# One fused kernel (attention, dense MLP, routed experts): queries and keys loaded one token per partition, one copy and quartered score products per attention unit, weight low parts on VectorE, and a new plan of the order

## The chip, the cores and the metric

The kernel runs on one core of one Trainium2 chip. The metric is the device time of one execution in microseconds (us), lower is better. In the profile PE is TensorE (the matrix unit; PEld is its weight load), DVE is VectorE, ACT is ScalarE, POOL is GpSimd, and SP is SyncE, which here only starts DMAs.

## What is computed

Three layers follow each other. All inputs and outputs are float32; 2304 tokens (4 sequences of 576) have 8 heads of 64 numbers, 512 in all.

```
scores = q @ k.T / 8                       # per head
mask   = (0 <= pos_q - pos_k < 64)         # a sliding window of 64 keys
attn   = softmax(where(mask, scores, -1e9))
x      = attn @ v                          # 2304 x 512
h = x @ w_in                               # 512 -> 2048
g = where(h > 0, h, exp(min(h, 0)) - 1)
x = g @ w_out                              # 2048 -> 512
e = argmax(x @ w_gate + modality_bias[modality_id])      # one of 8 experts per token
out = gate * (relu(x @ w1[e]) @ w2[e])     # 512 -> 1024 -> 512
```

## The kernel before, in words

**Attention** is done in 36 units. Unit n is tile t = n // 2 of 128 tokens with four of the eight heads. A unit passes through these pieces (names as in the planner): `ld` and `lv` start the loads of k, q and v on SP's queue; `1p` transposes k and q on TensorE; `1k`, `1l`, `1q`, `1r` copy the result from PSUM into buffers KB (192 keys wide: the 64 keys before the tile and its 128) and QB; `2p` makes the scores; `2d` adds the mask and takes the maximum (VectorE, L387) and scales the maximum (L389); `2x` is the exponential with its sum (ScalarE, L396); `2n` the reciprocal (L402, L403); `2m` multiplies by it on GpSimd (L408); `3p`, `3a` transpose the probabilities (L428) and copy them (L433); `4p` multiplies by v; `4a`, `4d` split the result into a rounded part xh and the rest xl (L451, L456). After `2p`, GpSimd copies the last 64 keys to the front of KB for the next tile (`kw`, L415 to L421). There are two probability buffers, so two units are on the way at a time.

The k and q of a unit are loaded with two neighbouring tokens on one partition, k on partitions 0 to 63 and q on 64 to 127, in pieces of 512 bytes. The first 12 units (`pair`) are transposed into pairs of heads, by a transpose (L324) and a product with the identity (L325) for each head, and their scores are products of quarters of the array (64 rows by 64 columns, L373). The other 24 units are transposed whole (L327), copied in eight smaller copies (four on ScalarE L335, four on VectorE L337), and their scores are four full products (L377).

**The dense layer** works in groups g of 256 tokens (four units) and steps s of 256 of the 2048 hidden features, 72 steps in all. `f1` is x times w_in (L531 to L533: high times high, low times high, high times low), `fx`, `fe`, `fm` the activation (L563 or L561, L567, L571), `fh` rounds it (L575), `fl` takes the rest on GpSimd (L579), and `f2` is the product with w_out (L540 to L542). Both weight matrices are prepared once and stay resident. Each of the 16 pieces (8 of each matrix) is loaded as 8-byte numbers and made into float32 in two halves: `wa` on ScalarE (L484), three bit operations on VectorE (`wb`: L491, L493, L496), the rounded high part (`wc`, on ScalarE for the first 8 of 32 halves and on VectorE for the other 24, L337 CAST), and the low part (`wd`) on GpSimd (L514). A step needs its two pieces of w_in and w_out. So the first two groups go through the 16 steps at the pace at which weights are made; later groups find them ready.

**Gate and experts** follow: `g1` computes the gate's logits on VectorE (L609), tokens are sorted by expert, and nine slots of 256 or 384 tokens go through their expert's weights (`e1`, `e2`).

**What sets the order.** The program is a list of pieces, each with an engine, a cost, what it needs, a rank and buffers that it takes and frees. `plan` (L18) plays these through as engines that do one piece at a time, and the instructions are written in the order in which it starts them. Nothing else of the plan is in the program: each engine runs its own list in order, with semaphores for data and buffers only. So a wrong cost or a contention that the plan does not know shows as an engine that waits behind a blocked instruction. Where TensorE would sit idle before time 40 of the plan, products of the identity with itself (`fill`, L1190) are put in.

## Time and profile before

| | us |
|---|---|
| median of three runs | 817.78 |
| the three runs | 817.78, 805.19, 818.21 |
| span of the profiled execution, first to last instruction (its own time is not given beside it) | 806.1 |
| busy: PE / DVE / ACT / POOL | 769.9 / 508.1 / 329.6 / 265.3 |

The profile is of one execution. Its span lies 0.9 us above the fastest run and 12.1 us below the slowest. Three stages are told apart below by the start of two matmuls: A, to the first dense step (0 to 49.75 us); B, the 16 steps of the first two groups (to 190.5 us); C, the other 56 steps, the gate and the experts. In a table of windows, a row gives the stretch and its length, then the busy time (and number of instructions) of PE, PEld, DVE, ACT and POOL, the granted TensorE clock as a share, the mean busy share of the 16 DMA engines, and GB/s. A group's row gives line, engine, operation, output<-inputs, shapes and count, then the busy time and the mean of one in ns, then the idle time of the engine before it with what ended it. A row of the timeline gives start, duration, engine, line, operation and count.

### The profile page before, as it was taken

What the parts mean: (1) busy time and instruction counts of PE and PEld (TensorE: products, weight loads), DVE (VectorE), ACT (ScalarE), POOL (GpSimd) and SP (SyncE); (2) the same over time, 40 slices, a digit from 0 to 9 for tenths busy, and PEclk for the clock granted to TensorE, in tenths of its full rate; (3) what the DMA queues carried; (4) which work ended last, traced back from release to release, by engine and by line L of the source; (5) the groups of instructions that cost most, each with busy time, mean ns of one, the idle gap of its engine ahead of it and who ended that gap; (6) DMA issues with size and microseconds to landing.
All of it is one profiled execution on the core that took longest, in us unless ns stands there. A gap on an engine that the chain in (4) does not pass through costs nothing. (4 is left out here: it accounts for less than half of the span.)

```text
span 806.1 us, 14932 instructions
## 1 busy us (share of the span) xinstructions
PE 769.9 (96%) x5440; PEld 675.5 (84%) x5440; DVE 508.1 (63%) x1508; ACT 329.6 (41%) x818; POOL 265.3 (33%) x263
## 2 busy tenths in 40 slices
PE   9998978799999999999999999999999999999996
PEld 5676867688889899889889888898889999999995
DVE  2689899996988759559569569165876223522210
ACT  2666644444334364564553555234521112411211
POOL 2356565572342432332333324224214112100001
PEclk9999998989999999999999999999999999999998
DMA  7367881212002022121221110002605610100001
GB/s 195 104 178 224 248 323 55 66 27 79 27 7 73 14 54 67 40 76 31 40 74 33 41 40 2 1 27 60 229 1 178 214 54 29 54 22 6 27 27 41
DMA packets 82337, 62.30 MB, mean 77 GB/s; under 512 B 46577, under 2 KB 69251, under 8 KB 82123
## 3 DMA queue, kind: packets, MB, share of 16 engines
q1 hardware_dynamic: 78635, 51.50, 21.7%
q0 software_dynamic: 3616, 9.72, 3.6%
q8 instruction: 45, 0.74, 0.4%
q14 instruction: 41, 0.34, 0.2%
HBM read 51.05 MB, written 10.42 MB: 76 GB/s over the span
## 5 line engine op out<-in xcount | busy, mean ns | idle before, releaser
L531 PE MATMUL h<-xh,whi 128*128 128x256 f32 x576 | 167.2, 290 | 0.0
L533 PE MATMUL h<-xh,wlo 128*128 128x256 f32 x576 | 163.5, 284 | 1.0 <-POOL wlo L514 1.0
L532 PE MATMUL h<-xl,whi 128*128 128x256 f32 x576 | 163.5, 284 | 0.0
L579 POOL TENSOR_TENSOR g<-e,g 128x512 fp32r<-128x512 f32 x72 | 101.0, 1404 | 170.6 <-ACT g L575 158.2
L540 PE MATMUL y<-whi,g 128*128 128x512 f32 x288 | 118.7, 412 | 4.9 <-ACT g L575 4.9
L542 PE MATMUL y<-whi,g 128*128 128x512 f32 x288 | 114.7, 398 | 3.6 <-POOL g L579 3.6
L541 PE MATMUL y<-wlo,g 128*128 128x512 f32 x288 | 113.5, 394 | 0.0
L531 PEld LDWEIGHTS h<-xh,whi 128*128 128x128 f32 x576 | 110.9, 192 | 2.6 <-PE p_rk L637 0.7
L532 PEld LDWEIGHTS h<-xl,whi 128*128 128x128 f32 x576 | 111.0, 193 | 1.1
L533 PEld LDWEIGHTS h<-xh,wlo 128*128 128x128 f32 x576 | 110.8, 192 | 1.2 <-POOL wlo L514 1.2
L609 DVE CUSTOM_DVE_ANT_0 lgs<-ysb,wgb 128x512 bf16<-128x512 f32 x96 | 77.7, 810 | 1.9
L575 ACT ACTIVATE g<-e 128x512 fp32r<-128x512 f32 x72 | 45.3, 630 | 73.5 <-DVE e L571 70.6
L531 PE MATMUL h<-xh,ehi 128*128 128x256 f32 x256 | 72.6, 283 | 0.6 <-ACT xh L900 0.6
L532 PE MATMUL h<-xl,ehi 128*128 128x256 f32 x256 | 72.6, 284 | 0.6 <-DVE xl L910 0.6
L533 PE MATMUL h<-xh,elo 128*128 128x256 f32 x256 | 72.5, 283 | 0.0
L940 DVE SCALAR_TENSOR_TENSOR g<-h,g 128x512 fp32r<-128x512 f32 x32 | 22.1, 689 | 77.2 <-ACT g L935 77.1
L396 ACT ACTIVATE sm<-sm,st 128x128 f32<-128x128 f32 x144 | 56.2, 392 | 34.2 <-DVE st L389 34.1
L542 PEld LDWEIGHTS y<-whi,g 128*128 128x128 f32 x288 | 54.8, 190 | 18.1 <-POOL g L579 5.8
L571 DVE SCALAR_TENSOR_TENSOR e<-e,h 128x512 f32<-128x512 f32 x72 | 49.1, 683 | 30.8 <-ACT e L567 25.2
L540 PEld LDWEIGHTS y<-whi,g 128*128 128x128 f32 x288 | 55.1, 191 | 15.1 <-ACT g L575 5.8
L567 ACT ACTIVATE e<-e 128x512 f32<-128x512 f32 x72 | 45.3, 629 | 47.7 <-DVE e L563 47.0
L935 ACT ACTIVATE g<-h 128x512 fp32r<-128x512 f32 x32 | 19.1, 596 | 109.6 <-PE h L533 104.8
(226 smaller groups left out, 1607.0 us busy)
## 6 DMA issues: line engine op xcount, KB each, us to landing
raw<-in_moe_w_in_dram SPq DMA_DIRECT2D x16, 512.0 KB, 5.6
raw<-in_moe_w_out_dram SPq DMA_DIRECT2D x16, 512.0 KB, 5.6
wraw<-in_moe_w_dram SPq DMA_DIRECT2D x16, 512.0 KB, 12.1
v<-in_v_dram SPq DMA_DIRECT2D x58, 128.0 KB, 2.7
kq<-in_k_dram SPq DMA_DIRECT2D x28, 128.0 KB, 3.0
kq<-in_q_dram SPq DMA_DIRECT2D x28, 128.0 KB, 3.1
yd<-ysb SPq DMA_DIRECT2D x12, 256.0 KB, 2.9
wgb<-wgt SPq DMA_DIRECT2D x1, 2048.0 KB
```

The source lines that it names most:

```text
L396: act(out=sm[:, h], in_=sm[:, h], func=AF.Exp, bias=st[:, 1, h:h + 1], scale=0.125, accum_out=st[:, 2, h:h + 1])
L531: mm(hs[c], w[0][:, d, f], xh, start=d == 0, stop=False)
L532: mm(hs[c], w[0][:, d, f], xl, start=False, stop=False)
L533: mm(hs[c], w[1][:, d, f], xh, start=False, stop=d == 3)
L540: mm(y, gh[:, m], w[0][:, c], start=first and c == 0, stop=False)
L541: mm(y, gh[:, m], w[1][:, c], start=False, stop=False)
L542: mm(y, gl[:, m], w[0][:, c], start=False, stop=last and c == 1)
L567: act(out=e, in_=e, func=AF.Exp, scale=-1.0 if on_act(g) else 1.0)
L571: dve.scalar_tensor_tensor(out=e, in0=e, scalar=-1.0, in1=H.pop((g, s)), op0=ALU.add, op1=ALU.max)
L575: act(out=a[:, 0], in_=EL[g, s], func=AF.Copy)
L579: pool.tensor_tensor(out=a[:, 1], in0=EL.pop((g, s)), in1=a[:, 0], op=ALU.subtract)
L609: dve.tensor_tensor_reduce(out=lgs, in0=y, in1=wgb[:, e], scale=1.0, scalar=0.0, op0=ALU.mult, op1=ALU.add, accum_out=GT[t][:, e:e + 1])
```

## The change

One copy of `ld` and `1p` serves all units now: k and q are loaded one token per partition, in pieces of 256 bytes, each unit is transposed whole by four transposes, and one copy on ScalarE (`1e`) puts k and q into KQ, which holds the unit's tile and the tile before it (two slots, t % 2). So nothing has to be copied from one tile to the next (`kw`, `qz` are gone). The scores of all units are products of quarters of the array (`2p`, L357 in the changed kernel), into two PSUM buffers of pool ps. The scaling of the maximum is folded into the mask instruction, so L389 goes. Of the 32 weight halves, the low part of 26 is taken on VectorE (LE) and that of 6 on GpSimd; the high part of 28 is cast on ScalarE and that of 4 on VectorE (HE). The first six dense steps write the activation back into PSUM and take its low part on VectorE (VIA). `fx` runs on ScalarE in seven groups of nine in place of four (FXA). The planner gets other costs, ranks and edges, and a resource L of one piece at a time, which the two-input pieces of GpSimd and VectorE take. It is only in the plan; no instruction waits for it.

```diff
-    KQC = 0.73
-    NPR = 12
-    QE = 'ACT'
-    KE = 'DVE'
-    G1R = 45.66
-    XBL = 8.0
-    SGL = -10.97
-    SG = 9.4
+    KQC = 1.2
+    G1R = 35.77
+    XBL = 6.5
+    SGL = 4.46
+    SG = 26.38
     FG = 0.3
...
-    LV = -19.5
-    UR = (0.71, 1.24)
-    HE = range(8, 32)
-    FXA = (1, 4, 7, 8)
-    YX = (1, 6, 7)
-    LG = 6.36
+    LV = -20.92
+    UR = (0.63, 2.97)
+    HE = range(28, 32)
+    LE = range(26)
+    VIA = range(6)
+    E1 = "ACT"
+    FXA = (1, 2, 3, 4, 6, 7, 8)
+    YX = (1, 2, 6, 7)
+    LG = 16.15
...
-    LOOK = 12
-    EK = ("ACT", "ACT", "DVE", "DVE")
+
+    L = {"L": 1}
...
-        u["kq"] = u["kq"].rearrange("p j h d -> p (j h d)").rearrange("p (h x d) -> p h x d", x=2, d=D)
-        # two tokens next to each other on a partition: k on partitions 0:64, q on 64:128
         for j, src in enumerate((k, q)):
-            for off, n, b, s in runs(t * 128, 128):
-                nc.sync.dma_start(out=u["kq"][64 * j + off // 2:64 * j + (off + n) // 2].rearrange("p h x d -> p h (x d)"),
-                                  in_=src[b, 4 * qd:4 * qd + 4, s:s + n, :].rearrange("h (p x) d -> p h (x d)", x=2))
+            load(u["kq"][:, j], src, t * 128, qd)
...
         for j in range(4):
-            if pair(t, qd):
-                x = a[:, j // 2 * 2:j // 2 * 2 + 2, j % 2]
-                T(p[0:64, j], x[:, 0], ident)
-                mm(p[64:128, j], x[:, 1], ident, start=True, stop=True)
-            else:
-                T(p[:, j], a[:, j].rearrange("p x d -> p (x d)"), ident)
...
+            T(p[:, j], a[:, j // 2, j % 2 * 2:j % 2 * 2 + 2].rearrange("p h d -> p (h d)"), ident)
...
-    # head by head: rows 0:64 hold the window of queries 0:64, rows 64:128 that of queries 64:128
-    def a1k(t, qd, b, eng):
-        p, K = U[t, qd]["p1"], KB[qd]
-        for x, r in enumerate(HALF):
-            put(eng, even_odd(K[HALF[b], :, 64 - 64 * b:192 - 64 * b], x), p[r, :, 0:64])
...
-    # the first units: pairs of heads as the transposes leave them, one product per head and half of the queries
-    def pair(t, qd):
-        return 2 * t + qd < NPR
-
-    def a1kk(t, qd, eng):
-        put(eng, even_odd(KB[qd][:, 0:2, 64:192]), U[t, qd]["p1"].rearrange("p (i x) c -> p i x c", x=2)[:, :, :, 0:64])
-
-    def a1qq(t, qd, eng):
-        put(eng, even_odd(QB[qd][:, 0:2, :]), U[t, qd]["p1"].rearrange("p (i x) c -> p i x c", x=2)[:, :, :, 64:128])
...
+    def a1e(t, qd, eng):
+        put(eng, KQ[qd][:, :, t % 2], U[t, qd].pop("p1"))
+
+
+    def window(t, qd, z, i, b):
+        a = KQ[qd][HALF[z], i]
+        if b:
+            return a[:, t % 2]
+        a = a.rearrange("p s (x c) -> p (s x) c", x=2)
+        return a[:, 1:3] if t % 2 else a[:, 0:4:3]
...
     def a2p(t, qd):
         u = U[t, qd]
-        p = u["p2"] = ps.tile([128, 4, 128], F32, tag="ps", name="p_s")
-        if pair(t, qd):
-            # the halves of the array work side by side, each on a bank of its own
-            p = u["p2"] = p, h_tile().rearrange("p a b -> p (a b)").rearrange("p (a b) -> p a b", b=128)
-            for i in range(2):
-                for b, r in enumerate(HALF):
-                    for z in range(2):
-                        mm(p[z][r, i], QB[qd][HALF[z], i, r], KB[qd][HALF[z], i, 64 * b:64 * b + 128],
-                           start=True, stop=True)
-            return
-        for h in range(4):
-            mm(p[:, h], QB[qd][:, h], KB[qd][:, h, 0:128], start=True, stop=True)
+        p = u["p2"] = [ps.tile([128, 2, 128], F32, tag="ps", name="p_s") for _ in range(2)]
+        for i in range(2):
+            for b, r in enumerate(HALF):
+                for z in range(2):
+                    mm(p[z][r, i], KQ[qd][HALF[z], 2 + i, t % 2, r], window(t, qd, z, i, b), start=True, stop=True)
...
         for h in (2 * i, 2 * i + 1):
-            src = p[h % 2][:, h // 2] if pair(t, qd) else p[:, h]
-            dve.tensor_tensor_reduce(out=sm[:, h], in0=src, in1=masks[:, mask_of(t), :], scale=1.0, scalar=-3.0e38,
-                                     op0=ALU.add, op1=ALU.max, accum_out=st[:, 0, h:h + 1])
-        dve.tensor_scalar(out=st[:, 1, 2 * i:2 * i + 2], in0=st[:, 0, 2 * i:2 * i + 2],
-                          scalar1=-0.125, scalar2=None, op0=ALU.mult)
+            dve.tensor_tensor_reduce(out=sm[:, h], in0=p[h % 2][:, i], in1=masks[:, mask_of(t), t % 2], scale=-0.125,
+                                     scalar=3.0e38, op0=ALU.add, op1=ALU.min, accum_out=st[:, 0, h:h + 1])
...
-            act(out=sm[:, h], in_=sm[:, h], func=AF.Exp, bias=st[:, 1, h:h + 1], scale=0.125,
-                accum_out=st[:, 2, h:h + 1])
+            act(out=sm[:, h], in_=sm[:, h], func=AF.Exp, bias=st[:, 0, h:h + 1], scale=-1.0,
+                accum_out=st[:, 1, h:h + 1])
...
-    def akw(t, qd):
-        K = KB[qd]
...
-        pool.tensor_copy(out=K[0:64, :, 0:64], in_=K[0:64, :, 128:192])
...
-        pool.tensor_tensor(out=lo[:, c], in0=CV[kind, i][:, z].bitcast(F32), in1=hi[:, c], op=ALU.subtract)
...
+        eng = pool if lo_eng(kind, i, z) == "POOL" else dve
+        eng.tensor_tensor(out=lo[:, c], in0=CV[kind, i][:, z].bitcast(F32), in1=hi[:, c], op=ALU.subtract)
+
+    def lo_eng(kind, i, z):
+        return "DVE" if (2 * i + (kind == "o")) * 2 + z in LE else "POOL"
...
+    def via_psum(g, s):
+        return g * NP + s in VIA
...
     def f1m(g, s):
         e = EL[g, s]
-        dve.scalar_tensor_tensor(out=e, in0=e, scalar=-1.0, in1=H.pop((g, s)), op0=ALU.add, op1=ALU.max)
+        h = H[g, s] if via_psum(g, s) else H.pop((g, s))
+        dve.scalar_tensor_tensor(out=h if via_psum(g, s) else e, in0=e, scalar=-1.0, in1=h, op0=ALU.add, op1=ALU.max)
...
     def f1h(g, s):
         a = G[g, s] = g_tile()
-        act(out=a[:, 0], in_=EL[g, s], func=AF.Copy)
+        act(out=a[:, 0], in_=H[g, s] if via_psum(g, s) else EL[g, s], func=AF.Copy)
 
     def f1l(g, s):
-        a = G[g, s]
-        pool.tensor_tensor(out=a[:, 1], in0=EL.pop((g, s)), in1=a[:, 0], op=ALU.subtract)
+        a, e = G[g, s], EL.pop((g, s))
+        if via_psum(g, s):
+            dve.tensor_tensor(out=a[:, 1], in0=H.pop((g, s)), in1=a[:, 0], op=ALU.subtract)
+        else:
+            pool.tensor_tensor(out=a[:, 1], in0=e, in1=a[:, 0], op=ALU.subtract)
...
+            w2p = [("2p", n - 2)] if back else []
+
+            room = [("f1", n // 4 - 3, NP - 1)] if n >= 12 else []
+            add(("1p", n), "PE", 0.55, a1p, *u, rank=r - 1000, deps=[("ld", n)] + w2p + room,
+                need={"ps": 1}, free={} if early else {"ld": 1}, lat=0.25)
+            e = e1_eng(n)
+            add(("1e", n), e, 0.49 if e == "ACT" else 0.6, a1e, *u, e, rank=r, deps=[("1p", n)] + w2p, free={"ps": 1})
+            add(("2p", n), "PE", 0.7, a2p, *u, rank=r - 1000, deps=[("1e", n)], need={"ps": 2, "P": 1}, lat=0.25)
             for i in range(2):
-                add(("2d", n, i), "DVE", 0.475, a2d, *u, i, rank=r, deps=[("2p", n) if i == 0 else ("2d", n, 0)],
-                    free=({"ps": 1} | ({"h": 1} if pair(*u) else {})) if i else {})
+                add(("2d", n, i), "DVE", 0.53, a2d, *u, i, rank=r, deps=[("2p", n) if i == 0 else ("2d", n, 0)],
...
-            add(("2n", n), "DVE", 0.17, a2n, *u, rank=r, deps=[("2x", n, 0), ("2x", n, 1)])
-            add(("2m", n), "POOL", 1.0, a2m, *u, rank=r, deps=[("2n", n)])
-            if t + 1 < NTILE:
-                add(("kw", n), "POOL", 0.55 if pair(units[n][0] + 1, qd) else 0.97, akw, *u, rank=r + 0.5, deps=[("2p", n)])
...
+            add(("2m", n), "POOL", 1.05, a2m, *u, rank=r, deps=[("2n", n)], need=L, free=L)
...
-                        deps=[("wb",) + w + (z, x - 1) if x else ("wa",) + w + (z,)], free={"w": 1} if x == 2 else {})
-                add(("wc",) + w + (z,), hi_eng(*w, z), 0.52 if hi_eng(*w, z) == "ACT" else 0.34, w_c, *w, z, rank=r,
-                    deps=[("wb",) + w + (z, 2)] + ([("wc",) + w + (0,)] if z else []), need={} if z else {"w": 2})
-                add(("wd",) + w + (z,), "POOL", 1.23, w_d, *w, z, rank=r, deps=[("wc",) + w + (z,)],
-                    free={"w": 1} if z else {})
...
+                        deps=[("wb",) + w + (z, x - 1) if x else ("wa",) + w + (z,)], need=L, free=L | ({"w": 1} if x == 2 else {}))
+                lk = L if he == "DVE" else {}
+                add(("wc",) + w + (z,), he, 0.52 if he == "ACT" else 0.34, w_c, *w, z, rank=r,
+                    deps=[("wb",) + w + (z, 2)] + ([("wc",) + w + (0,)] if z else []), need=lk | ({} if z else {"w": 2}), free=lk)
+                add(("wd",) + w + (z,), le, 1.23 if le == "POOL" else 0.6, w_d, *w, z, rank=r, deps=[("wc",) + w + (z,)],
+                    need=L, free=L | ({"w": 1} if z else {}))
...
+                if via:
+                    add(("fl",) + k, "DVE", 0.6, f1l, *k, rank=r - 900, deps=[("fh",) + k], free={"h": 1})
+                else:
+                    add(("fl",) + k, "POOL", 1.23, f1l, *k, rank=r - 900, deps=[("fh",) + k], need=L, free=L | {"e": 1})
...
         caps = {"w": 33, "ps": 4, "h": 2, "y": 1, "P": 2, "v": 3, "ld": 2, "PA": 1, "X": 3, "e": 2, "g": 3,
-                "gs": 3, "ix": 5}
+                "gs": 3, "ix": 5, "L": 1}
```

The order itself comes out of the planner. On TensorE, the stretch after the score products of the first two units stands so before (p_t is the transposed unit, kqv its loaded k, q and v, kb and qb the buffers KB and QB; a unit's transposes are eight matmuls):

```order
L373 MATMUL h<-kb_110,qb_108 64x128
L324 MATMUL p_t<-ident,kqv 64x128
L325 MATMUL p_t<-ident,kqv 64x128
L324 MATMUL p_t<-ident,kqv 64x128
L325 MATMUL p_t<-ident,kqv 64x128
L324 MATMUL p_t<-ident,kqv 64x128
L325 MATMUL p_t<-ident,kqv 64x128
L324 MATMUL p_t<-ident,kqv 64x128
L325 MATMUL p_t<-ident,kqv 64x128
L1190 MATMUL fill<-ident 128x128 x2
```

and so in the change (L331 transposes, L357 scores, L393 the probabilities' transposes, L407 the product with v):

```order
L357 MATMUL p_s<-kq_108 64x128 x8
L331 MATMUL p_t<-ident,kqv 128x128 x4
L1165 MATMUL fill<-ident 128x128 x4
L331 MATMUL p_t<-ident,kqv 128x128 x4
L393 MATMUL p_a<-ident,sm 128x128 x4
L357 MATMUL p_s<-kq_107 64x128 x8
L407 MATMUL p_o<-PA,kqv 64x64 x8
```

Each unit's eight transposes in two forms became four in one form; the order of the units is the same. The first dense step stands after nine units' transposes before, after eight in the change.

On VectorE, a stretch in which weights are made stands so before (wf is the float32 under construction, raw the loaded numbers, whi the high part, qb a copy of q for a unit, e the activation):

```order
L563 TENSOR_SCALAR e<-h 128x512
L337 CAST whi<-wf 128x512
L491 TENSOR_SCALAR wf<-wf 128x512
L337 COPY qb_107<-p_t 64x4x32 x2
L493 SCALAR_TENSOR_TENSOR wf<-raw,wf 128x512
L571 SCALAR_TENSOR_TENSOR e<-e,h 128x512
L496 SCALAR_TENSOR_TENSOR wf<-raw,wf 128x512
```

and so in the change (L456, L458, L461 are the bit operations, L480 the low part wlo, L548 the activation, L421 the rest xl of a unit):

```order
L421 TENSOR_TENSOR xl<-p_o,xh 128x2x128
L548 SCALAR_TENSOR_TENSOR e<-e,h 128x512
L461 SCALAR_TENSOR_TENSOR wf<-raw,wf 128x512
L480 TENSOR_TENSOR wlo<-wf,whi 128x512
L458 SCALAR_TENSOR_TENSOR wf<-raw,wf 128x512
L480 TENSOR_TENSOR wlo<-wf,whi 128x512
L461 SCALAR_TENSOR_TENSOR wf<-raw,wf 128x512
L456 TENSOR_SCALAR wf<-wf 128x512 x2
```

The casts and the copies of q have left VectorE's list, and the low parts stand in it, and between the last bit operation of a half and its low part stand two to 17 other instructions.

On GpSimd, the list in the same stage stands so before (g is the activation's low part, sm the probabilities):

```order
L514 TENSOR_TENSOR wlo<-wf,whi 128x512 x2
L579 TENSOR_TENSOR g<-e,g 128x512
L514 TENSOR_TENSOR wlo<-wf,whi 128x512
L421 COPY kb_109<-kb_109 64x4x64
L514 TENSOR_TENSOR wlo<-wf,whi 128x512 x2
L579 TENSOR_TENSOR g<-e,g 128x512
```

and so in the change (L480 the low parts that stay, L559 g, L385 the probabilities):

```order
L385 TENSOR_TENSOR sm<-sm,st 128x512
L559 TENSOR_TENSOR g<-e,g 128x512 x3
L480 TENSOR_TENSOR wlo<-wf,whi 128x512 x2
L559 TENSOR_TENSOR g<-e,g 128x512
L480 TENSOR_TENSOR wlo<-wf,whi 128x512
L559 TENSOR_TENSOR g<-e,g 128x512
L480 TENSOR_TENSOR wlo<-wf,whi 128x512 x2
```

Most low parts and all copies of keys are gone from it.

## Rows read from the trace of the kernel before

**Rows 1.** The page's first line.

```profile
span 806.1 us, 14932 instructions
```

**Rows 2.** Windows of the stages A, B and C.

```profile
0.00:49.75 49.75, 46.48 (x403) 29.93 (x403) 25.44 (x113) 24.89 (x87) 18.04 (x35) 1.00 0.59 157
49.75:190.50 140.75, 124.56 (x922) 105.25 (x922) 128.63 (x281) 72.23 (x182) 81.67 (x73) 0.95 0.49 152
190.50:806.10 615.60, 598.88 (x4120) 540.31 (x4118) 354.04 (x1115) 232.44 (x551) 165.59 (x155) 1.00 0.18 54
```

**Rows 3.** Waits in stage A: total us, times, longest.

```profile
DVE kb L337 <- PE p_t L325: 17.8, 7, 6.3
```

**Rows 4.** Timeline of TensorE: score products of three pairs of units.

```profile
13.22 0.47 PE L373 MATMUL p_s<-kb,qb 64*64 64x128 f32 x1
...
22.91 0.32 PE L373 MATMUL p_s<-kb,qb 64*64 64x128 f32 x1
...
32.70 0.32 PE L373 MATMUL p_s<-kb,qb 64*64 64x128 f32 x1
```

**Rows 5.** Timeline of TensorE: transposes of a paired unit, what follows, and a plain unit's.

```profile
53.46 0.30 PE L324 MATMUL p_t<-ident,kq 128*64 128x128 f32 x1
...
55.84 0.66 PE L428 MATMUL p_a<-ident,sm 128*128 128x128 f32 x4
...
109.22 0.60 PE L327 MATMUL p_t<-ident,kq 128*128 128x128 f32 x4
```

**Rows 6.** Groups by shape, whole run: score products, 12 paired and 24 plain units.

```profile
L377 PE MATMUL p_s<-kb,qb 128*128 128x128 f32 x192 | 27.5, 288 | 5.0 <-DVE qb L337 4.9
...
L373 PE MATMUL p_s<-kb,qb 64*64 64x128 f32 x96 | 8.7, 307 | 0.0
```

**Rows 7.** Window from the first to the last activation product of stage B.

```profile
57.40:181.90 124.50, 108.31 (x781) 92.26 (x782) 119.60 (x249) 64.03 (x157) 76.23 (x68) 0.95 0.51 160
```

**Rows 8.** Groups of VectorE, 57 to 182 us.

```profile
L496 DVE SCALAR_TENSOR_TENSOR wf<-raw,wf 128x512 int32<-128x512 int32 x28 | 24.2, 868 | 0.1
L493 DVE SCALAR_TENSOR_TENSOR wf<-raw,wf 128x512 int32<-128x512 int32 x28 | 23.6, 852 | 0.1
L491 DVE TENSOR_SCALAR wf<-wf 128x512 int32<-128x512 int32 x27 | 20.6, 770 | 1.0 <-ACT wf L484 0.9
L337 DVE CAST whi<-wf 128x512 fp32r<-128x512 f32 x24 | 18.0, 748 | 0.0
L571 DVE SCALAR_TENSOR_TENSOR e<-e,h 128x512 f32<-128x512 f32 x16 | 10.9, 680 | 0.3
L389 DVE TENSOR_SCALAR st<-st 128x2 f32<-128x2 f32 x14 | 6.6, 469 | 0.5
...
L337 DVE COPY qb<-p_t 64x128 f32<-64x128 f32 x16 | 4.6, 287 | 0.2
```

**Rows 9.** Timeline of VectorE.

```profile
101.73 1.67 DVE L493 SCALAR_TENSOR_TENSOR wf<-raw,wf 128x512 int32<-128x512 int32 x1
...
104.05 0.69 DVE L496 SCALAR_TENSOR_TENSOR wf<-raw,wf 128x512 int32<-128x512 int32 x1
104.66 0.42 DVE L491 TENSOR_SCALAR wf<-wf 128x512 int32<-128x512 int32 x1
```

**Rows 10.** Timeline of GpSimd at the same time.

```profile
101.55 1.30 POOL L514 TENSOR_TENSOR wlo<-wf,whi 128x512 fp32r<-128x512 f32 x1 [0.36 <-DVE whi L337]
```

**Rows 11.** Groups of GpSimd, 57.4 to 181.9 us.

```profile
L514 POOL TENSOR_TENSOR wlo<-wf,whi 128x512 fp32r<-128x512 f32 x28 | 41.4, 1478 | 24.4 <-DVE whi L337 19.9 <-ACT whi L335 4.2 <-DMA kq<-in_k_dram 0.4
L579 POOL TENSOR_TENSOR g<-e,g 128x512 fp32r<-128x512 f32 x15 | 21.9, 1460 | 15.5 <-ACT g L575 15.5
```

**Rows 12.** Group of ScalarE, whole run: a copy of 128x512 from PSUM.

```profile
L433 ACT ACTIVATE PA<-p_a 128x512 f32<-128x512 f32 x36 | 21.4, 595 | 29.1 <-PE p_a L428 29.1
```

**Rows 13.** Waits, whole run: low parts behind high parts cast on ScalarE.

```profile
POOL wlo L514 <- ACT whi L335: 6.5, 3, 4.2
```

**Rows 14.** DMA issues: count, KB each, median us from issue to landing.

```profile
v<-in_v_dram SPq DMA_DIRECT2D x58, 128.0 KB, 2.7
kq<-in_k_dram SPq DMA_DIRECT2D x28, 128.0 KB, 3.0
```

More of the change, by code (lines that the diff above doesn't have):

```diff
@@ L150, in fused @@
     ident = const.tile([128, 128], F32, name="ident")
-    masks = const.tile([128, 3, 128], F32, name="masks")
-    QB = [const.tile([128, 4, 128], F32, name=f"qb{i}") for i in range(2)]
-    KB = [const.tile([128, 4, 192], F32, name=f"kb{i}") for i in range(2)]
+    masks = const.tile([128, 3, 2, 128], F32, name="masks")
+    KQ = [const.tile([128, 4, 2, 128], F32, name=f"kq{i}") for i in range(2)]
     wgb = const.tile([128, E, DM], F32, name="wgb")
@@ L310, in u_v @@
         load(a[:, 1], v, t * 128, qd)
+        if t % 2:
+            load(a[:, 0], v, t * 128 - 64, qd)
+            return
+        load(a[0:64, 0], v, t * 128, qd)
         if t:
-            load(a[:, 0], v, t * 128 - 64, qd)
+            load(a[64:128, 0], v, t * 128 - 64, qd)
         else:
-            pool.memset(a[0:64, 0], 0.0)
-            nc.sync.dma_start(out=a[64:128, 0], in_=v[0, 4 * qd:4 * qd + 4, 0:64, :].rearrange("h p d -> p h d"))
+            pool.memset(a[64:128, 0], 0.0)
     def a1p(t, qd):
@@ L1063, in program @@
+            add(("4a", n), "ACT", 0.28, a4a, *u, rank=r,
                 deps=[("4p", n)] + ([("4a", n - 1)] if n % 4 else []))
@@ L1086, in program @@
                 yb = {"ps": 2} if g == 1 else {"y": 1}
-                add(("f1",) + k, "PE", 2.6, f1p, *k, rank=r + 1.5,
-                    deps=[("wd", "i", s, 0), ("wd", "i", s, 1)] + [("4d", 4 * g + x) for x in range(4)] + ([("f1", g, s - 1)] if s else [("f1", g - 1, NP - 1)] if g == NG - 1 else []),
+                via = via_psum(g, s)
+                add(("f1",) + k, "PE", 2.9, f1p, *k, rank=r + 1.5,
+                    deps=[("wd", "i", s, 0), ("wd", "i", s, 1)] + [("4d", 4 * g + x) for x in range(4)] + ([("f1", g, s - 1)] if s else [("f1", g - 1 - (g < NG - 1), NP - 1)] if g > 1 else []),
                     need={"h": 1}, free=({"X": 1} if s == NP - 1 else {}) | ({"w": 2} if g == NG - 1 else {}), lat=0.22)
@@ L1136, in program @@
             add(("eh", j), "ACT", 0.95, e_hi, j, rank=j - 600.0, deps=[("el", j)], need={"w": 2})
[L1137 removed]
+            add(("ex", j), "DVE", 1.14, e_lo, j, rank=j - 600.0, deps=[("eh", j)], need=L, free=L)
         for s in range(NS):
```

108 lines of the change are left out of this document (40 added, 68 removed).

## The prediction, on record before the changed kernel ran

> **What bounds the kernel now.** I read the windows by stage first. In stage C TensorE is busy for 598.9 of 615.6 us [rows 2]: there only TensorE's own work counts, and little of its time is idle. In stage B it is busy for 124.6 of 140.8 us, 16.2 us idle, at a mean granted clock of 0.95, so part of its busy time is at the lower of its two levels, 1.2 in place of 2.4 GHz; in stage A, 3.3 us of 49.75 are idle, but with the planner's `fill` products among the busy ones. So the time that can come back lies in A and B, and in work that TensorE no longer does.
>
> Stage B next. From its first to its last activation product VectorE is busy for 119.6 of 124.5 us [rows 7], ScalarE for 64, GpSimd for 76: VectorE sets the pace at which weights, and with them steps, become ready. Much of that busy time is not work. The reader is to see in the timeline an L493 that took 1.67 us from 101.73 on, beside a GpSimd low part that ran from 101.55 for 1.30 us [rows 9, 10]; of two that nothing disturbed, the same kind took 0.69 and L491 took 0.42. The groups show it in their means: 868, 852 and 770 ns for the three bit operations and 748 ns for the cast, while L571, which has one input in PSUM, stays at 680 [rows 8]. So VectorE instructions whose tensors are all in SBUF stand still while GpSimd runs.
>
> Stage A last. VectorE waited 17.8 us in seven waits for a unit's transposes [rows 3]. The score products of pairs of units start at 13.22, 22.91 and 32.70 us [rows 4]: a loop of 9.7 us for two units, and the transposes of one paired unit hold TensorE from 53.46 to 55.84, 2.38 us, those of a plain one 0.60 us [rows 5]. A loop contains two such sets.
>
> **The change, part by part.** Durations are those of the profiled execution, so the sum is made against its span of 806.1 us [rows 1]. Its own time is not listed; the runs of 805.19, 817.78 and 818.21 us lie 0.9 us below to 12.1 above that span, so what lies around a span, or differs between executions, is bounded by these two.
>
> *Transposes, stage A.* Nine paired units stand before the first step; each becomes 2.38 - 0.60 = 1.78 us cheaper, 16.0 us in all. If all of it were on the path, A would shorten by 16 (and by up to 18 if the ninth unit's set, now behind the first step, goes whole). The wait of 17.8 us [rows 3] says that most of it is. Against that, ScalarE, busy for 24.9 us in A [rows 2], must now do the copy of each unit whole, 0.595 us [rows 12], where VectorE and ScalarE shared it, and the exponentials, the normalisation and the loads stay in the loop. I take 12, between bounds of 4 and 18, nearer to the row of the wait. There are fewer `fill` products; they stand in idle time and cost nothing.
>
> *VectorE, stage B.* Removed: 20 of the 24 casts, 20 x 0.748 = 15.0 us; all L389, 6.6; the copies of q, 4.6; together 26.2 [rows 8]. Added: 26 low parts. Their nearest row is the bit operation of the same size with two inputs, 0.61 us from start to start (104.05 to 104.66, rows 9), so 15.9 us; and six low parts of the activation, 3.7; together 19.6. Stalls of what stays: L491 27 x (0.770 - 0.42) = 9.5, L493 28 x (0.852 - 0.69) = 4.5, L496 28 x (0.868 - 0.69) = 5.0, together 19.0 us [rows 8, 9]. GpSimd ran 28 + 15 two-input pieces there [rows 11]; 6 low parts and 9 activation parts stay, 15 of 43, so I let 65% of the stalls go, 12.3 us, and let the new low parts pay the rest at the same rate, 26 x 0.17 x 0.35 = 1.6. Hand-offs: the high part of 20 more halves now comes from ScalarE between two pieces of VectorE. When GpSimd waited for a high part from ScalarE it waited 6.5 us in 3 times, 2.2 each [rows 13]. In the new order between two and 17 other VectorE instructions stand between a half's last bit operation and its low part, six in the median (counted in the order), and ScalarE, idle for half of the stage [rows 7], has a cast of that size (0.595, rows 12) done in about the time of one. I take 0.2 each, 5 us for 26, between 0 and the 57 that 2.2 would make. Sum: -26.2 + 19.6 - 12.3 + 1.6 + 5 = -12.3 us, bounded by -25 and, without any relief, +3. While VectorE is the bound, B shortens by this; what is late next is TensorE's own work of the stage. The lower clock follows TensorE's idle stretches, so its cost goes with them and I add no term.
>
> *GpSimd, DMA and SP.* GpSimd loses 26 low parts of 1.478 us [rows 11] and all copies of keys; it only released others. SP issues the same two DMAs per unit for k and q, moved past no queue that feeds a step, and one more short one for v in even tiles. A page says otherwise of the pieces: the Trainium skill, "DMA: Bandwidth & Descriptors", section Specifications, wants at least 512 B for line rate, and the change goes from 512 to 256 B. The rows point the other way: v, already in 256-byte pieces, lands after 2.7 us, k in 512-byte pieces after 3.0, for the same 128 KB [rows 14]. I take nothing; the rule's case is a rival below.
>
> *Stage C.* The score products of a plain unit take 27.5 / 24 = 1.15 us, of a paired one 8.7 / 12 = 0.73 [rows 6]. Some 20 of the 24 plain units lie in C, where TensorE is the bound: 20 x 0.42 = 8.4, taken as 8. The copies, L389, `kw` and the move of `fx` to ScalarE are hidden there under TensorE (VectorE is busy for 354 of 615.6 us, ScalarE for 232); without that cover nothing of them would be dearer than before. Three units that stood before the 17th step now stand behind it; that moves TensorE's work from B to C, and I count it as zero. The new edges and ranks hold attention back more; the 16.7 us of idle time in C could grow or shrink, +-6.
>
> Sum: 806.1 - 12 - 12 - 8 = 774 us of span. With 3 us for what the runs show around it I forecast **777 us**, 5.0% under the median of 817.78 and 3.5% under the fastest run. About 2% is what a measurement of this kernel can tell from no change.
>
> **The rivals.** *1. The lock stays.* The resource L is only in the plan; no wait in the program keeps GpSimd and VectorE apart, and drift of a microsecond undoes it. For it: that L493 started 0.18 us after the GpSimd piece [rows 9, 10]. Against it: there are 65% fewer such pieces whatever the order. Without relief B changes by -26.2 + 19.6 + 5 + 4.4 (26 x 0.17) = +3, and the span is 806 - 12 + 3 - 8 = 789, as time 789 to 801.
>
> *2. Small pieces are slow.* If k and q took twice as long to land, 6.0 in place of 3.0 us, each of three loops of stage A would wait 3 us more: 783 of span, 783 to 795. Rows 14 speak against it. This is what "DMA: Bandwidth & Descriptors" of the Trainium skill would make of the change.
>
> *3. Slower: VectorE waits for ScalarE's casts.* VectorE does its list in order. If each of the 26 low parts blocks it for the 2.2 us of [rows 13], every bit operation and activation behind it waits too: 57 us in place of 5, 774 + 52 = 826 us. It decides from 2 us per hand-off on, where the gain is lost and 2% with it ((806 + 16 - 774) / 26 + 0.2). For it: ScalarE takes 20 casts more and all unit copies. Against it: it is idle for half of the stage, and at least two other VectorE instructions stand between.
>
> *4. More comes back.* All of the transposes (16 to 18 us in A) and all stalls: then TensorE itself bounds stage B. 806 - 17 - 22 - 8 = 759 us.
>
> **How the numbers follow.** The forecast has 65%, rival 1 13%, rival 2 5%, rival 3 3%, rival 4 14%. The predicted time is that of the forecast, 777. The range runs from 756, below rival 4, to 800, near the end of rival 1; it leaves out about 2 in 10: rival 3, and the outer ends of the bounds of A and of stage C. Faster by over 2% (under 801 against the median): forecast, rivals 2 and 4 and half of rival 1, 90%; within 2%: the rest of rival 1 and a little of the others, 7%; slower: rival 3, 3%.
>
> **What would show it.** Stage A: the first dense step near 38 us, the loop of two units near 7, and VectorE's wait for transposes at a few us. Stage B: 16 steps in about 128 us, VectorE's bit operations at means near 0.45 for the shift and 0.75 for the other two, low parts near 0.7, and a clock of 1.00. Stage C: near 608 us. I would be wrong if the first step still came after 45 us (then transposes were not on the path), if VectorE's list showed waits for ScalarE's casts of over 20 us, if the means stayed at 0.77 and 0.86, or if TensorE waited in stage C for attention units that the new edges hold back.

## The result: 5.0% was forecast, 4.4% came, by other terms than mine

The changed kernel takes **774.5 us** (median of four runs, 773.49 to 776.23). The kernel before took 813.3 us in the four runs beside it (805.19 to 818.21). The ratio is **0.956, 95% interval 0.951 to 0.961**. The forecast was 777 us, the range 756 to 800. The span of the profiled execution went from 806.1 [rows 1] to 773.2 us, 32.9 us less; it took 775.0 us itself, 1.8 more than its span. One reservation for the experiments: the profile of e7 is of an execution slower than its other runs (832.6 us, their median 826.8), so its stage lengths are told and nothing rests on them alone.

First the three stages of the changed kernel, in the columns of [rows 2]; the 17th dense step starts at 138.67.

```profile
span 773.2 us, 14786 instructions
...
0.00:29.18 29.18, 24.98 (x313) 20.53 (x313) 15.96 (x83) 22.30 (x77) 12.76 (x27) 1.00 0.86 210
29.18:138.67 109.49, 102.88 (x795) 89.43 (x792) 101.17 (x216) 68.05 (x154) 34.88 (x24) 1.00 0.61 186
138.67:773.20 634.53, 610.01 (x4425) 541.54 (x4425) 316.83 (x1017) 237.24 (x561) 164.70 (x144) 0.99 0.20 56
```

Stage A is 20.6 us shorter (forecast 12), stage B 31.3 (forecast 12.3), and stage C is **18.9 us longer** (forecast 8 shorter). The total came out right because these misses cancel, which is luck.

In stage A VectorE's wait for transposes is gone. What answers to [rows 3] is, in the waits up to 29.18 us, a wait of VectorE for score products and one of ScalarE for the transposes:

```profile
DVE sm L367 <- PE p_s L357: 7.3, 3, 5.7
ACT kq L335 <- PE p_t L331: 5.0, 3, 3.2
```

The longest of the first, 5.7 us, is at the start, before there is any unit. TensorE's timeline shows the loop of two units: 5.8 and 5.9 us, then 8.5, where [rows 4] had 9.7 and 9.8, and a unit's transposes take 0.66, where [rows 5] had 2.38.

```profile
6.01 0.74 PE L357 MATMUL p_s<-kq 64*64 64x128 f32 x16
6.69 0.66 PE L331 MATMUL p_t<-ident,kqv 128*128 128x128 f32 x4
...
11.79 0.67 PE L357 MATMUL p_s<-kq 64*64 64x128 f32 x16
...
17.72 0.67 PE L357 MATMUL p_s<-kq 64*64 64x128 f32 x16
...
25.17 0.72 PE L331 MATMUL p_t<-ident,kq 128*128 128x128 f32 x4 [0.89 <-DMA kq<-in_k_dram]
...
26.25 0.67 PE L357 MATMUL p_s<-kq 64*64 64x128 f32 x16
```

The third loop is the one in which TensorE waited for a load, 0.89 us at 25.17.

In stage B these groups of VectorE (29.18 to 138.67) answer to [rows 8], and those of GpSimd to [rows 11]:

```profile
L458 DVE SCALAR_TENSOR_TENSOR wf<-raw,wf 128x512 int32<-128x512 int32 x30 | 22.1, 743 | 0.0
L461 DVE SCALAR_TENSOR_TENSOR wf<-raw,wf 128x512 int32<-128x512 int32 x30 | 20.5, 691 | 0.0
L480 DVE TENSOR_TENSOR wlo<-wf,whi 128x512 fp32r<-128x512 f32 x24 | 20.5, 863 | 0.0
L456 DVE TENSOR_SCALAR wf<-wf 128x512 int32<-128x512 int32 x30 | 12.9, 452 | 3.1 <-ACT wf L449 3.1
...
L337 DVE CAST whi<-wf 128x512 fp32r<-128x512 f32 x4 | 3.0, 755 | 0.0
```

```profile
L559 POOL TENSOR_TENSOR g<-e,g 128x512 fp32r<-128x512 f32 x8 | 20.9, 2613 | 35.0 <-ACT g L552 35.0
L385 POOL TENSOR_TENSOR sm<-sm,st 128x512 f32<-128x512 f32 x6 | 7.4, 1233 | 33.9 <-DVE st L380 17.3 <-ACT whi L335 10.6 <-ACT wf L449 4.0
L480 POOL TENSOR_TENSOR wlo<-wf,whi 128x512 fp32r<-128x512 f32 x5 | 6.7, 1337 | 7.8 <-PE p_t L331 7.8
```

The shift's mean fell from 770 to 452 ns and the last bit operation's from 868 to 691: that stall is nearly gone. The new low parts, at 863, are dearer than the 0.61 us I took: undisturbed they take 0.68, and some still stand behind a GpSimd piece, as at 64.76, in the timelines of VectorE and of GpSimd. The mean of 2613 ns of GpSimd's `g` hides two pieces of some 6 us; the last section comes to them.

```profile
63.55 0.68 DVE L480 TENSOR_TENSOR wlo<-wf,whi 128x512 fp32r<-128x512 f32 x1
...
64.76 1.79 DVE L480 TENSOR_TENSOR wlo<-wf,whi 128x512 fp32r<-128x512 f32 x1
```

```profile
64.28 1.72 POOL L559 TENSOR_TENSOR g<-e,g 128x512 fp32r<-128x512 f32 x1 [8.40 <-ACT g L552]
```

The rows of loads answer to [rows 14]: in 256-byte pieces k and q land after 3.2 and 3.0 us, the medians of the whole run.

```profile
v<-in_v_dram SPq DMA_DIRECT2D x42, 128.0 KB, 3.2
kq<-in_k_dram SPq DMA_DIRECT2D x28, 128.0 KB, 3.2
kq<-in_q_dram SPq DMA_DIRECT2D x28, 128.0 KB, 3.0
```

### The profile page after: what moved, and what is told of

Read it like the earlier page. It is cut to its first block, busy times and chain, and to the rows that moved or that the text cites. A ratio compares the mean times of both kernels' runs of the same rounds, so it can differ in the third digit from the quotient of the medians.

```text
span 773.2 us, 14786 instructions
## 1 busy us (share of the span) xinstructions
PE 737.9 (95%) x5528; PEld 651.5 (84%) x5528; DVE 434.0 (56%) x1314; ACT 327.6 (42%) x790; POOL 212.3 (27%) x194
## 5 line engine op out<-in xcount | busy, mean ns | idle before, releaser
L559 POOL TENSOR_TENSOR g<-e,g 128x512 fp32r<-128x512 f32 x66 | 100.4, 1521 | 227.7 <-ACT g L552 197.6
L548 DVE SCALAR_TENSOR_TENSOR e<-e,h 128x512 f32<-128x512 f32 x66 | 45.2, 684 | 85.3 <-ACT e L539 70.4
L552 ACT ACTIVATE g<-e 128x512 fp32r<-128x512 f32 x66 | 41.7, 632 | 49.9 <-DVE e L548 49.6
L513 PEld LDWEIGHTS y<-wlo,g 128*128 128x128 f32 x288 | 54.7, 190 | 9.2
L533 ACT ACTIVATE e<-h 128x512 f32<-128x512 f32 x56 | 33.1, 592 | 66.8 <-PE h L505 62.1
```

The source lines that it names most:

```text
L513: mm(y, gh[:, m], w[1][:, c], start=False, stop=False)
L533: act(out=e, in_=H[g, s], func=AF.Relu, scale=-1.0)
L548: dve.scalar_tensor_tensor(out=h if via_psum(g, s) else e, in0=e, scalar=-1.0, in1=h, op0=ALU.add, op1=ALU.max)
L552: act(out=a[:, 0], in_=H[g, s] if via_psum(g, s) else EL[g, s], func=AF.Copy)
L559: pool.tensor_tensor(out=a[:, 1], in0=e, in1=a[:, 0], op=ALU.subtract)
```

## The experiments

Each ratio is against the kernel before; the changed kernel's is 0.956, and 0.01 is 8 us. Stage lengths are of the profiled execution. In all runs but e10 to e12 the planner places every piece anew, so what a run measures is its setting together with another order; e5 and e9 show that an order alone can be worth several points.

**e1_attention_only.** The changed kernel, VectorE's part undone.

```
-    HE = range(28, 32)
-    LE = range(26)
-    VIA = range(6)
-    FXA = (1, 2, 3, 4, 6, 7, 8)
+    HE = range(8, 32)
+    LE = range(0)
+    VIA = range(0)
+    FXA = (1, 4, 7, 8)
```

> The changed kernel with VectorE's part undone: low parts of the weights all on GpSimd, 24 casts of the high parts on VectorE, no low parts of activations through PSUM, fx on ScalarE in four groups as before; the attention part, the new planner numbers and the lock stay. Theory 1 (VectorE sets the pace of stage B, so its lighter list gave most of the 31 us that stage B lost): slower than the changed kernel by 12 to 20 us, 787 to 795 us, all of it in stage B. Theory 2 (the gain is TensorE's own work: transposes 21.7 and scores 11 us shorter, 32.7 of the 32.0 us of busy time that went; VectorE's part only fills in): within 5 us of the changed kernel, 772 to 780 us.

826.8 us, ratio 1.0135 [1.008, 1.019]: slower than before. A 31.5, B 132.4, C 661.6. B alone is 23 us longer than in the changed kernel, as theory 1 has it, but 27 more were lost in C, which neither theory named. Theory 2 is out. In B, TensorE waited once for 22.5 us, for an activation on VectorE (`e`, L548). In TensorE's timeline:

```profile
78.52 0.28 PE L505 MATMUL h<-xh,wlo 128*128 128x256 f32 x1
101.28 0.55 PE L503 MATMUL h<-xh,whi 128*128 128x256 f32 x1 [22.48 <-DVE e L548]
```

All that time VectorE was at work without a pause, until 99 us on bit operations, casts and three small pieces of the gate that stand before the activation in its list. (The expectation of e8, below, puts this wait into stage C, behind a row of gate logits from 246 to 261 us. The trace does not have it there: in C no wait of TensorE is longer than 2.6 us.) What C shows is a stretch in which TensorE is often idle and its granted clock near the lower of its two levels (1.2 in place of 2.4 GHz), and the gate's weights (`wgb`) are fetched only at 214 us, against 134 in the changed kernel:

```profile
190.00:220.00 30.00, 22.69 (x184) 16.47 (x184) 9.48 (x53) 12.10 (x44) 6.71 (x6) 0.54 0.46 126
```

**e8_attention_gate_early.** e1 with four ranks of the gate as before.

```
-    G1R, SGL, SG, LG = 35.77, 4.46, 26.38, 16.15
+    G1R, SGL, SG, LG = 45.66, -10.97, 9.4, 6.36
```

> The kernel of e1_attention_only with the four ranks of the gate (SG, SGL, LG, G1R) as before, so that the gate's weights come early. In e1 they were fetched at 214 us, 80 us later than in the changed kernel, 20 logits then stood on VectorE in front of an activation, and TensorE waited 22.5 us. Theory 1 (this is the 27 us that e1's stage C is longer than the changed kernel's): 797 to 805 us, so that the attention part alone is worth 1.5 to 2.5% against before. Rival (without VectorE's part the attention part gives nothing, whatever the gate's place): 815 to 828 us.

802.2 us, ratio 0.992 [0.988, 0.995]. The gate's weights come at 59 us, C is 630.9, the clock from 190 to 220 us is 0.94, and 2.2 points of e1's loss are back. The time is in theory 1's range, its reason is not (the 22.5 us stood in B), and against before it is 0.8%, not 1.5 to 2.5. So the gate's four ranks cost e1 its stage C; by which wait is not shown. The attention part with the new plan is worth 0.8% by itself. B is still 138.5 us long.

**e2_vector_only** and **e7_edges_only.** The kernel before with VectorE's part; it needs the planner's new edges, so e7 has these alone.

```
+            room = [("f1", n // 4 - 3, NP - 1)] if n >= 12 else []
-   ... else [("f1", g - 1, NP - 1)] if g == NG - 1 else [])
+   ... else [("f1", g - 1 - (g < NG - 1), NP - 1)] if g > 1 else [])
```

> The kernel before with VectorE's part alone: 26 low parts of the weights on VectorE, casts on VectorE only for the last four halves, six low parts of activations through PSUM, fx on ScalarE in seven groups, and the new edges between units and groups, without which no complete order comes out. Theory 1: faster than before by 12 to 20 us, 793 to 801 us, in stage B. Theory 2: within 5 us of before, 808 to 818 us.

> The kernel before with the new edges of the planner alone (a unit's transposes wait for the group three ahead, a group's first step for the last of the one two ahead): three units fewer stand before the 17th step, 12 in place of 15. Theory 1 (the moves on VectorE gave e2_vector_only its 12 us in stage B): stage B within 4 us of 140.75, stage C within 4 of 615.6. Rival (the three units did: about 2.9 us of VectorE and 3 us of TensorE each): stage B 128 to 133 us, stage C 624 to 631, the total within 6 us of before, 808 to 820 us, and so the moves on VectorE alone gave nothing.

e2: 811.1 us, ratio 0.995 [0.990, 1.000]: theory 2's number, but not for its reason. B is 128.7 (12.0 shorter), C 631.4 (15.8 longer). e7: 826.8 us, **1.020** [1.012, 1.028], beyond what either theory expected: the edges by themselves cost 2 points. Against that base VectorE's part is worth 2.5 points, give or take one, some 20 us, also without the new attention. In e7's profile, with the reservation above, B is 139.8 us and C 636.4: VectorE is busy for 5.5 us less in B than before and idle for 4.5 more, so there the three units that left B did not shorten it.

**e3_whole_transposes.** The kernel before with `NPR = 0` for `NPR = 12`.

> The kernel before with the plain form for all units: whole transposes and undivided scores, four copies per unit, nothing else changed. Per unit the transposes go from 2.38 to 0.60 and the scores from 0.73 to 1.15 us of TensorE. Theory 1 (A is a chain through the transposes and the copies): the first dense step 6 to 10 us earlier than 49.75, since the two more copies take part of it back, 800 to 807 us. Theory 2 (TensorE's work alone counts): 12 units by 1.36 us = 16 us, 796 to 798 us.

824.4 us, ratio 1.012 [1.007, 1.018]: both theories missed. A shrank to 34.36 us, by 15.4, almost all of the 16.0 that nine sets of transposes save (as in the changed kernel, eight sets and not nine stand before the first step). But B grew to 160.6 and C to 627.7. In B VectorE is busy for 149.8 us, and TensorE is idle for 30 at a clock of 0.91. TensorE's time saved early bought nothing here, where VectorE's weights were late.

**e4_low_parts_on_gpsimd.** The changed kernel with `LE = range(0)`.

> The changed kernel with the 26 low parts of the weights back on GpSimd, all else as changed. My sum in the prediction makes the move of the low parts itself a loss on VectorE: 15.9 of work, 1.6 of stalls and 5 of hand-offs against 12.3 of relief; by it this kernel is 5 to 10 us faster, 764 to 770 us. Rival (what counts is that a low part on GpSimd stalls VectorE for 0.3 to 0.5 us in each of the bit operations beside it, and takes 1.3 in place of 0.68 us between a weight and its step): 5 to 12 us slower, 779 to 787 us, with means of the bit operations back near 0.77 to 0.87 us.

792.0 us, ratio 0.971 [0.967, 0.974], 12 us slower than the changed kernel: my sum for this move has the wrong sign, and the rival's upper bound is met. A is 2.3 us longer (31.52; nine sets of transposes stand there, not eight), B 20.8 (130.3), C 7.0 shorter (one step's second product more, some 3 us of TensorE, stands in B). Groups of VectorE and of GpSimd, two waits, and one piece of GpSimd, in its stage B:

```profile
L461 DVE SCALAR_TENSOR_TENSOR wf<-raw,wf 128x512 int32<-128x512 int32 x30 | 29.8, 1006 | 0.0
L458 DVE SCALAR_TENSOR_TENSOR wf<-raw,wf 128x512 int32<-128x512 int32 x30 | 23.8, 808 | 0.1
L456 DVE TENSOR_SCALAR wf<-wf 128x512 int32<-128x512 int32 x29 | 15.3, 550 | 1.8 <-ACT wf L449 1.8
...
L535 DVE TENSOR_SCALAR e<-h 128x512 f32<-128x512 f32 x8 | 5.5, 684 | 8.4 <-PE h L505 8.4
```

```profile
L480 POOL TENSOR_TENSOR wlo<-wf,whi 128x512 fp32r<-128x512 f32 x30 | 41.3, 1394 | 26.8 <-ACT whi L335 14.4 <-DVE whi L337 4.6 <-PE h L505 4.2
```

```profile
PE y L514 <- POOL g L559: 9.4, 1, 9.4
DVE e L535 <- PE h L505: 8.4, 3, 6.1
```

```profile
95.58 12.37 POOL L559 TENSOR_TENSOR g<-e,g 128x512 fp32r<-128x512 f32 x1 [6.01 <-ACT g L552]
```

The bit operations cost 68.9 us in place of 55.5, so stalls give back 13.4 of the 20.5 us that the low parts no longer take; with other pieces VectorE's busy time is the same, 101.0 against 101.2. What is new is that it is *idle* for 29.3 us in place of 8.3. Of these, 16.9 us ended with TensorE (0.2 in the changed kernel). TensorE's longest wait, 9.4 us, is for the `g` above: one subtraction of GpSimd that lasted 12.37 us while VectorE did 21 bit operations in a row, at their undisturbed times.

**e6_casts_on_vector.** The changed kernel with `HE = range(8, 32)`.

> The changed kernel with 20 of the casts back on VectorE, so 24 as before; all else as changed. Theory 1 (VectorE sets the pace of stage B; a cast adds 0.42 us undisturbed, 0.75 in the mean of before): 20 casts add 8 to 15 us to stage B, 782 to 790 us. Rival (the hand-off to ScalarE costs VectorE as much as the cast itself): within 3 us, 772 to 778 us, and VectorE's waits for ScalarE's casts vanish.

784.9 us, ratio 0.972 [0.966, 0.978], 13 us more; theory 1. In the profiled execution, the fastest of the four (span 778.1), B is 117.1, 7.6 more (theory 1 had 8 to 15), VectorE 6.2 busier.

**e10_low_parts_twice, e11_transposes_twice, e12_casts_twice.** The order of all else is untouched; one kind of work is doubled on its engine.

```
+        for _ in range(1 if eng is pool else 2): eng.tensor_tensor(out=lo[:, c], ...)    # e10
+        for j in list(range(4)) * 2: T(p[:, j], ...)                                     # e11
+        for _ in range(2 if hi_eng(kind, i, z) == "ACT" else 1): put(...)                # e12
```

> The changed kernel with each of the 26 low parts on VectorE computed twice, in the same order of all else: 26 x 0.68 us more on VectorE, 24 of them in stage B. Theory 1 (VectorE sets the pace of stage B): 12 to 17 us slower, 787 to 792 us, in stage B. Rival (TensorE has become the bound there, busy for 102.9 of 109.5 us, and VectorE's 8.3 us of idle time take the rest): 775 to 781 us.

> The changed kernel with each unit's four whole transposes done twice, in the same order of all else: 36 x 0.55 to 0.60 us more on TensorE, about 8 units in stage A, 6 in B and 22 in C. Theory 1 (A is a chain through the transposes and C is TensorE's own work; B is VectorE's): A 4 to 5 us and C 12 to 13 us longer, B not: 790 to 793 us. Rival (in A the chain runs through ScalarE and VectorE, and TensorE there has `fill` products to spare): C alone, 786 to 788 us.

> The changed kernel with each of the 28 casts of high parts on ScalarE done twice, in the same order of all else: 28 x 0.6 us more on ScalarE, and each hand-off from a half's last bit operation to its low part 0.6 us longer. Theory 1 (the hand-offs are covered by other work of VectorE and cost nothing): within 4 us of the changed kernel, 772 to 779 us. Rival (VectorE waits for ScalarE's casts, rival 3 of the prediction in small): 10 to 17 us slower, 785 to 792 us.

e10: 792.9 us, ratio 0.979 [0.973, 0.984]. A 29.63, B 125.1, C 634.1: B is 15.6 us longer for 24 x 0.68 = 16.3 us more on VectorE. Its window of stage B:

```profile
29.63:154.74 125.11, 112.18 (x795) 95.30 (x792) 118.89 (x241) 68.04 (x154) 26.55 (x24) 0.93 0.52 159
```

VectorE sets the pace of stage B nearly one for one, and is the bound in the changed kernel still; the clock dips to 0.93 as TensorE waits.

e11: 779.1 us, ratio 0.961 [0.956, 0.967], 4 us more; both theories missed. The groups of the transposes rose by 15.6 us in the run (from 18.9 and 3.0):

```profile
L331 PE MATMUL p_t<-ident,kq 128*128 128x128 f32 x256 | 32.4, 275 | 2.6 <-DVE xl L421 1.6 <-DMA kq<-in_k_dram 1.1
L331 PE MATMUL p_t<-ident,kqv 128*128 128x128 f32 x32 | 5.1, 313 | 0.0
```

A grew by 1.0, B not at all, C by 3.5, where TensorE was 8.4 us busier: its idle time in C, 24.5 us in the changed kernel, took the rest. So TensorE's own work is no longer worth its full price even in C, and in A the transposes no longer bind.

e12: 780.5 us, ratio 0.963 [0.957, 0.969], 5 to 6 us more, in B 4.75: a hand-off that is 0.6 us longer costs 0.17 us. Nearer to theory 1, just beyond its bound.

**e5_no_lock** and **e9_no_lock_gate_early.** The planner's lock made plentiful, alone and with the gate's four ranks as in e8.

```
-                "gs": 3, "ix": 5, "L": 1}
+                "gs": 3, "ix": 5, "L": 99}
```

> The changed kernel with the resource L of the planner made so plentiful that it holds nothing back; no instruction is added or taken away, only the order is another. Theory 1 (the lock in the plan keeps GpSimd's pieces away from VectorE's bit operations): the disturbed bit operations rise from 13 of 56 towards the 50 of 76 of before, 6 to 12 us slower, 780 to 787 us. Rival (drift undoes a plan of this kind, only the number of pieces on GpSimd counts): 772 to 778 us.

> The kernel of e5_no_lock (the planner's lock holds nothing back) with the four ranks of the gate as before. In e5 the gate's weights were fetched at 194 us, in the changed kernel at 134 us; stage C was 24 us longer, with TensorE idle and at a clock of 0.88 from 146 to 217 us. Theory 1 (the lock's 33 us came from where it happens to put the gate, not from the port): with the weights fetched earlier, 776 to 788 us. Rival (the lock itself keeps the engines apart and is worth most of it): 797 to 807 us.

e5: 807.2 us, ratio **1.001** [0.997, 1.005]: all of the gain is lost by a resource that exists in the plan alone, and neither theory came near. e9: 799.5 us, 0.986 [0.978, 0.994]: 1.5 points of it go with the gate's four ranks (its weights come at 142 us, in e5 at 194), 3.0 points do not; theory 1 is out. But the rival's mechanism does not show. Of VectorE's bit operations in stage B, 28 of 89 overlapped a GpSimd piece of over 0.9 us in the changed kernel, 27 of 88 in e5, 36 of 88 in e9, against 57 of 87 before; and what these and the low parts took beyond their undisturbed 0.42 and 0.68 us is 7.6, 7.5 and 7.7 us (20.2 before, for the bit operations alone). GpSimd's two-input pieces took 10.0, 7.9 and 13.4 us beyond 1.4 each. So VectorE loses no more to GpSimd without the lock. What differs is VectorE's idle time in stage B, 8.3 us against 20.0 (117.4 - 97.4, e5) and 22.9 (e9; all that e9 lost against the changed kernel, it lost in B, 131.0 us long), and in e5 a stretch right after it with TensorE often idle and its clock low:

```profile
28.40:145.79 117.39, 105.62 (x813) 91.76 (x810) 97.35 (x217) 73.72 (x167) 33.51 (x25) 0.96 0.57 168
145.79:216.60 70.81, 61.47 (x520) 51.31 (x518) 30.44 (x118) 34.15 (x99) 18.11 (x16) 0.88 0.30 83
```

By these counts the lock works as a device that orders pieces, more than as one that keeps two engines apart. Which of the many places where the orders differ is worth the 3.0 points stays open.

## Why the prediction held, and where its steps failed

**The bound.** "VectorE sets the pace" of stage B is shown by e10 (15.6 us of 16.3) and by e3. That only TensorE's own work counts in stage C is not, in the changed kernel at least: e11 priced 8.4 us there at 3.5, and by that price (an estimate) the 8 us of cheaper score products were worth 3 to 4.

**Stage A: right mechanism, too small.** e3 shows the transposes on the path with 15.4 of 16.0 us; I had discounted them to 12, "nearer to the row of the wait". e4 hints at a term I did not have: with the low parts off GpSimd, where a unit's normalisation (L385) runs as well, A is 2.3 us shorter, one set of transposes among it. If the two add up, the rest, 49.75 - 29.18 - 15.4 - 2.3 = 2.9 us, goes with the smaller parts, which were not tried apart.

**Stage B: -12.3 forecast, -31.3 measured.** By the groups of the windows of B, VectorE's terms were:

| term | forecast | measured |
|---|---|---|
| casts, L389, copies out of the transposes | -26.2 | -28.4 (15.0 + 7.1 + 6.3) |
| low parts, of weights and activations | +21.2 | +24.6 |
| stalls of the three bit operations | -12.3 | -15.8 |
| hand-offs to ScalarE; VectorE's idle time | +5 | -3.8 |
| attention pieces of three units that moved to C | 0 | -8.8 |

The measured terms make -32.2, small groups the rest. Each priced piece of work was near. **The step that failed** is "Three units that stood before the 17th step now stand behind it ... I count it as zero". What it is worth as a whole, e7 shows: the edges alone cost 2 points, some 16 us. By the table they took 8.8 us of VectorE out of B (1.1 of it is that L402 got shorter, 270 to 157 ns), and they put TensorE's time into C. That the 8.8 us shortened B is bookkeeping and not shown: in e7's profile B was no shorter without the units. The hand-off term failed too: no L480 waited (idle 0.0 in its group). Hand-offs are not free, though: 0.6 us more on each costs 4.75 us (e12). Rival 3 did not happen.

My sum also made the move of the low parts a loss of about 10 us of VectorE (15.9 + 1.6 + 5 - 12.3). e4, with the order that comes with it, has it as a gain: 20.8 us of stage B, 12 us of the whole. The relief was sized well, 13.4 us. What I had left out is the chain through GpSimd: "GpSimd loses 26 low parts ...; it only released others". It did not only release others: in e4 TensorE waited 9.4 us for one piece of it, and VectorE 16.9 us for TensorE.

**Stage C: -8 forecast, +18.9 measured.** TensorE is busy for 11.1 us more and idle for 7.8 more. The score products did get cheaper. Their group in C, and in the fence behind it that of the kernel before:

```profile
L357 PE MATMUL p_s<-kq 64*64 64x128 f32 x384 | 16.8, 281 | 1.4 <-DVE xl L421 1.2
```

```profile
L377 PE MATMUL p_s<-kb,qb 128*128 128x128 f32 x160 | 22.1, 281 | 0.4 <-DVE qb L337 0.3
```

That is 0.70 us for each of 24 units in place of 1.1 for each of 20, 5.3 less. But three more units stand there by the order (four, for the score products): the other three kinds of attention product add 4.9, the second products 4.1 (one step more, some 3 us), those with w_in and w1 1.0. These groups sum to 4.9 us more (small ones 0.2); the other 6.2 of the busy time is that the groups overlap less than before, and why is open. Of the added idle time 4.3 us stand before the products that rank the gate's tokens (`p_rk`, L617), which waited 8.7 us for VectorE in place of 4.4; before attention's products TensorE waited 3.8 us, 2.2 before, so the sign that I had named there hardly shows. The edges are what moved the units, and e7 prices them at 2 points when they stand alone. I had named that danger and given it +-6 us.

**The rivals.** "The lock stays" was right that no wait enforces the lock, and wrong that it then does little: e5. "Small pieces are slow" did not come at its price of 3 us in each of three loops; two loops took 5.8 and 5.9 us. It left a trace, though: in stage A the loads of kq whose landing is in the trace took, least, median and longest,

```profile
DMA to landing us min/median/max: 3.0/4.5/5.6
```

and TensorE waited 0.89 us for one in the loop of 8.5 us. In stage A of the kernel before it was

```profile
DMA to landing us min/median/max: 1.8/2.6/3.3
```

Whether the pieces did that, or the fuller DMA engines (a busy share of 0.86 in stage A in place of 0.59), was not tried apart. This is where the Trainium skill, "DMA: Bandwidth & Descriptors", section Specifications, wants 512 B for line rate; over the whole run pieces of 256 B landed after 3.2 and 3.0 us where those of 512 B took 3.0 and 3.1, and from 10 to 20 us, at a DMA share of 0.99, 247 GB/s were moved, where it was 256 at 0.98 before. The page "SBUF — State Buffer" of the Trainium skill, section "SBUF: two separate sides", says of the port that VectorE and GpSimd share that, where a VectorE piece has two inputs in SBUF and the GpSimd piece reads SBUF, whichever starts first holds it for its whole instruction. The trace agrees for most pieces: the low part at 64.76 ended 0.55 us after the GpSimd piece that started before it, and took 1.79 in place of 0.68 us. It does not agree for all; the last section counts both.

**Parts and whole.** Attention with the new plan is worth 0.8 points (e8), VectorE's part 0.5 (e2); together they give 4.4. Why so much more is not shown: each of these runs also has an order of its own, and e9 shows what that can move. A sum of terms against the kernel before gives the whole; it does not say what a part is worth.

## What to carry to other kernels

Before a saving is added up, ask which stage the displaced work lands in: a unit moved from one stage to the next is not a zero (the edges that did it cost 2 points alone). Double a suspected cost in an otherwise fixed order; that prices a bound in one run (16.3 us of VectorE gave 15.6, 8.4 us of TensorE gave 3.5). And where a planner sets the order, read a changed plan as a change of its own: a resource that no instruction knows moved this kernel by 4.5 points, 3.0 with the gate's ranks of before, as much as all of the new work.
